# A Mamba-2 scan fused with a low-rank mixer on one core: B, C and y of half the pairs turned as 32x32 squares on VectorE and through DRAM

## The chip, the cores and the metric

The kernel runs on one core of a Trainium2 chip. Its time is the device time of one execution in microseconds (us). Times of single instructions come from one profiled execution, read from the hardware profiler's trace; ns are marked. In the profile's words, PE is TensorE's matmul, PEld its weight load, DVE is VectorE, ACT is ScalarE, POOL is GpSimd, and SP is SyncE, whose queue (SPq) issues the kernel's DMAs.

## The reference, cut to what matters

Two stages follow one another. The first is a chunked scan (Mamba-2): 4 batches, 8 heads, 768 tokens, head dimension 32, state size 16, in chunks of 32 tokens. The second is a mixer on the scan's output, joined over heads to 256 columns: a low-rank mixing over the tokens (rank 32) and a channel MLP (256 to 1024 to 256, with ReLU).

```python
for c in range(seq // 32):                      # per batch and head
    M = (Cc @ Bc.T) * L                         # 32 x 32, decays below the diagonal
    y[c] = M @ xc + (Cc @ state) * exp(cum)     # within the chunk, and from the state
    state = decay_full * state + (Bc * decay_from_j).T @ xc
x = y.transpose(0, 2, 1, 3).reshape(4, 768, 256)
u = x + (x.transpose(0, 2, 1) @ U @ V).transpose(0, 2, 1)
out = u + relu(u @ w_ch1) @ w_ch2
```

All inputs and the output are float32.

## The kernel before, in words

**Tiles.** A batch's 768 tokens are cut into three pairs of two 128-token tiles. The 12 pairs are numbered k = 3 x batch + q. For each pair, B and C (16 columns for each of 8 heads, so 128 columns each) are loaded with tokens on partitions, decayed (`prep`, L463, into BC, and `decayed`, L475), and then turned so that (head, state) lies on the partitions: T holds, for tile i = 0, 1, the turned B and the turned C, 128x128 each. `turning` (L486) does this with four TensorE transposes into one PSUM bank (L497). ScalarE then copies the bank to T (L501) and writes Cm, the turned C under the two masks in `slot` that blank the odd or the even heads (L507). Three T and three Cm tiles are in rotation. `gram` (L521) multiplies B and C of T and Cm into the 32x32 grams, `mask` (L535) lays the causal mask over them, `state` and `update` (L554, L570) carry the state, `inter` (L637) and `intra` (L672) make y, and `yout` (L690) copies it on ScalarE to yT, which holds a batch's y with channels on partitions and tokens along the row: 128 x 2 x 768.

**The mixer of a batch** is made of `project` (L741: y, with tokens on partitions, by U), `mixed` (L755, by V) and `added` (L765, into yT); ScalarE copies what `project` gives to pT (L753), which `mixed` reads. `project` needs y turned back, with tokens on partitions. `ytokening` (L708) does that for a pair: four TensorE transposes into a bank (L714), and one copy of 128x512 to ytok, on ScalarE for batches 0 and 1 and on VectorE for batches 2 and 3. From then on the MLP goes over blocks of 256 tokens, three per batch: `split` (L780) cuts u into a near and a far part and their joint, `first` (L815, eight matmuls and a scaling), `second` (L822, four matmuls and a ReLU) and `third` (L833, two operations of VectorE) make a quarter of the hidden layer in three float32r parts, and `down` (L873) multiplies it by the second weights in pieces. The last pieces of a block add u, turn the result on VectorE in 32x32 squares and write it to the output in four DMAs (`vector.transpose` and L909). Batch 0's blocks are turned by TensorE and written in one DMA of 256 KB (L923), and its blocks 0 and 1 have a plain float32 hidden layer (`plain`, L802), whose pieces of `down` are called plain here, the others split. Every VectorE call is made through one helper, so the profile shows all of them at L169.

**PSUM** has eight banks, in three rotations: "w" 2, "x" 3 and "z" 3 (L130). A bank is handed out again when its last reader is done. The transposes use "w", as do the state and the projection; grams, intra and the MLP use "x" and "z".

**What sets the order.** Nothing is scheduled by a compiler: `follow` (L996) reads a plan, a long string of words, and issues each word's instructions at once, so the words' order is the order on every engine's queue. A word is a letter and numbers. For the scan the number n is the pair k = 3 + n, so that T3 is pair 6, the first of batch 2, and t5 is pair 8. For the mixer, the first number is a lag, and the batch is 1 - lag: f1.2.0 is `first` for batch 0, block 2, quarter 0, p-1 is `project` of batch 2, and p-2 that of batch 3.

| letter | word | engines |
|---|---|---|
| P, D | `prep`, `decayed` | VectorE (GpSimd for batch 0) |
| T (twice per pair) | `turning`: two transposes each; the second also makes the copy and Cm | PE, ACT |
| g; m, M | `gram`; half a mask each | PE; VectorE |
| s; u | `state`; `update` | PE; VectorE, ACT |
| i, n; y | `inter`, `intra`; `yout` | PE; ACT |
| t | `ytokens` | PE, ACT or VectorE |
| L, R, U, c | loads, the weights' splitting, the first weights in plain float32 | SP; VectorE, ACT; PE |
| p; x; a; S | `project`; `mixed`; `added`; `split` | PE, ACT; PE; VectorE; ACT, VectorE |
| f, e, h; d | `first`, `second`, `third`; one piece of `down` or `rows` | PE and ACT, h VectorE |

The engines work their queues in order; a DMA that must wait for something holds SP's queue behind it. The part of the code that decides how T is made, word for word:

```python
def turned(k):
    t = turns.setdefault(k, turning(k))
    for _ in range(2):
        next(t)
```

A T word runs two steps of the generator, up to its second `yield`.

Of the kernel before, what the change touches and what calls it, by code (L numbers as in the profile page):

```python
# [10 lines left out]
FP32 = mybir.dt.float32  # L11
# [3 lines left out]
WCOLS = 512  # L15
NWORDS = 12
PLAIN = 2
ROWS = 3
FOUR = 3

# [3 lines left out]
AF = mybir.ActivationFunctionType  # L24
# [19 lines left out]
        'U1.0.0 g0 U1.0.1 g1 m0 M0 c5 c4 m1 M1 c5 D1 s0 u0 U1.1.0 U1.1.1 U1.1.2 i0 n0 y0 c6 c6 '  # L44
        's1 c5 g2 c7 u1 R2 m2 c7 U1.1.3 M2 c8 c8 c7 U1.0.2 L4 U1.0.3 i1 n1 y1 c6 R1 R0 c8 R5 c9 '
        's2 c9 c9 n2 d1.0 L5 R6 u2 R0 d1.1 P3 S1.2 d1.0 R7 d1.0 i2 y2 R3 t1 R1 t0 R2 R5 d1.1 R4 '
        'f1.2.0 D4 T3 T3 P4 R7 R6 t2 f1.2.1 R3 D3 d1.1 f1.2.2 d1.0 R4 e1.2.0 d1.1 h1.2.0 e1.2.1 '
        'T4 f1.2.3 d1.0 T4 e1.2.2 e1.2.3 h1.2.1 P5 g3 p0 m3 M3 L6 d1.2 d1.2 d1.2 T5 L7 d1.2 L8 '
        'T5 h1.2.2 x0 h1.2.3 d1.2 a0.0 d1.2 d1.2 a0.1 S0.0 d1.2 g4 m4 s3 f0.0.1 D5 M4 f0.0.0 '
        'd1.2 d1.2 d1.2 e0.0.0 e0.0.1 u3 h0.0.0 f0.0.2 d1.2 h0.0.1 f0.0.3 e0.0.2 s4 u4 n3 h0.0.2 '  # L50
        'i3 e0.0.3 h0.0.3 d1.1 D6 S0.1 d1.2 d0.0 d0.0 y3 d0.0 d0.0 d0.0 S0.2 d0.0 d0.0 d0.0 D7 '
        'n4 s5 i4 d0.0 d0.0 g5 P7 y4 u5 P6 m5 M5 d0.0 d0.0 t3 D8 f0.2.1 f0.1.2 s6 n5 i5 y5 '
        'e0.1.2 u6 f0.2.0 f0.1.0 f0.1.3 h0.1.2 T7 e0.2.0 h0.2.0 e0.2.1 e0.1.3 h0.2.1 P8 T7 '
        'h0.1.3 f0.1.1 d0.2 f0.2.2 f0.2.3 e0.1.0 h0.1.0 e0.1.1 h0.1.1 e0.2.2 e0.2.3 h0.2.3 d0.1 '
        'd0.1 T6 T6 d0.1 d0.1 d0.1 t4 h0.2.2 t5 d0.1 d0.1 d0.1 d0.2 d0.2 d0.2 d0.2 d0.0 g7 m7 '
        'p-1 d0.2 d0.2 x-1 M7 a-1.0 a-1.1 s7 d0.2 u7 d0.1 d0.1 d0.1 g6 m6 d0.1 M6 d0.1 d0.2 d0.2 '
        'd0.2 d0.2 d0.2 S-1.0 T8 T8 i6 n6 y6 s8 n7 S-1.1 i7 y7 f-1.0.2 f-1.0.3 g8 e-1.0.2 '
        'e-1.0.3 m8 M8 f-1.1.0 f-1.0.1 h-1.0.3 h-1.0.2 f-1.0.0 f-1.1.1 e-1.1.0 e-1.0.0 e-1.0.1 '
        'h-1.1.0 h-1.0.1 e-1.1.1 f-1.1.2 h-1.0.0 d-1.0 S-1.2 f-1.1.3 e-1.1.2 h-1.1.2 d-1.0 d-1.0 '
        'd-1.0 d-1.0 f-1.2.0 u8 d-1.0 d-1.0 h-1.1.1 d-1.1 e-1.2.0 h-1.2.0 t6 e-1.1.3 f-1.2.2 '  # L60
        'd-1.1 d-1.1 d-1.0 h-1.1.3 e-1.2.2 h-1.2.2 d-1.1 d-1.1 d-1.1 d-1.1 d-1.1 i8 n8 t7 d-1.1 '
        'd-1.1 y8 d-1.1 t8 p-2 d-1.1 x-2 d-1.0 d-1.0 a-2.0 f-1.2.1 a-2.1 S-2.0 d-1.0 d-1.0 S-2.1 '
        'f-1.2.3 e-1.2.1 h-1.2.1 f-2.0.2 e-1.2.3 f-2.0.0 f-2.0.1 d-1.2 d-1.2 e-2.0.0 h-1.2.3 '
        'e-2.0.2 h-2.0.0 f-2.0.3 S-2.2 h-2.0.2 d-1.2 e-2.0.1 d-1.2 d-1.2 d-1.2 e-2.0.3 h-2.0.3 '
        'f-2.1.0 h-2.0.1 f-2.1.1 f-2.1.2 e-2.1.0 e-2.1.1 h-2.1.0 f-2.1.3 d-1.2 d-1.2 d-1.1 '
        'e-2.1.2 h-2.1.1 f-2.2.1 e-2.1.3 d-2.0 d-1.2 d-1.2 d-2.0 d-2.0 d-2.0 h-2.1.2 d-1.2 d-1.2 '
        'd-2.1 d-2.1 d-1.0 h-2.1.3 f-2.2.0 f-2.2.2 d-2.0 d-2.0 d-2.0 d-2.0 e-2.2.2 d-2.1 e-2.2.0 '
        'h-2.2.0 d-1.2 h-2.2.2 d-2.0 d-2.0 f-2.2.3 d-2.1 d-2.1 d-2.1 e-2.2.3 d-2.0 d-2.1 d-2.1 '
        'e-2.2.1 h-2.2.3 d-2.0 d-2.2 d-2.2 d-2.2 d-2.0 h-2.2.1 d-2.1 d-2.1 d-2.1 d-2.1 d-2.2 '
        'd-2.1 d-2.2 d-2.2 d-2.2 d-2.2 d-2.2 d-2.2 d-2.2 d-2.2 d-2.2 '),  # L70
}


# [1 line left out]
def kernel(  # L75
# [37 lines left out]
    NCB = DM // P  # L113
# [4 lines left out]
    NQ = NM // 2  # L118
    Q = 32
# [5 lines left out]
    att = ctx.enter_context(tc.tile_pool(name="att", bufs=2))  # L125
# [32 lines left out]
    class Kept:  # L158
# [6 lines left out]
        def __getattr__(self, name):  # L165
# [8 lines left out]
    vector = Kept(nc.vector)  # L174
# [53 lines left out]
    w1f = [w1all[:, c] for c in range(NQ)]  # L228
# [98 lines left out]
    for g in range(2):  # L327
# [3 lines left out]
        out=la.rearrange("p b c h -> p b h c"),  # L331
# [8 lines left out]
    slot = const.tile([P, 2], FP32)  # L340
# [115 lines left out]
    st = {}  # L456
# [29 lines left out]
    def turning(k, c=0, n=2, tag="w", engine=None, sooner=False):  # L486

        s = st[k]
        if c == 0:
            s["T"] = att.tile([P, 2, 2, P], FP32, tag="T", name="T", bufs=3)  # L490
            s["Cm"] = att.tile([P, 2, 2, P], FP32, tag="Cm", name="Cm", bufs=3)
        tp = bank(tag, 2, n, P)
        for i in range(2):
            for v in range(n):
                if i or v:
                    yield
                nc.tensor.transpose(out=tp[:, i, v],  # L497
                                    in_=s["BC"][:, i, c + v].rearrange("p h n -> p (h n)"),
                                    identity=ident)
        if sooner or not engine:  # L500
            nc.scalar.copy(out=s["T"][:, :, c:c + n], in_=tp)  # L501
        for i in range(2):
            if engine:
                engine.tensor_scalar(out=s["Cm"][:, i, c:c + n], in0=tp[:, 1],
                                     scalar1=slot[:, i, None], scalar2=None, op0=ALU.mult)
            else:
                nc.scalar.activation(s["Cm"][:, i, c:c + n], tp[:, 1], AF.Copy,  # L507
                                     scale=slot[:, i, None])
        if engine and not sooner:
            nc.scalar.copy(out=s["T"][:, :, c:c + n], in_=tp)  # L510
        yield

    def turn(*args):
        for _ in turning(*args):
            pass
# [192 lines left out]
    def ytokening(k, tag="w", copies=None):  # L708

        b, q = pairs[k]  # L710
        t = [bank(tag[0], 2, 2, P)] * 2 if len(tag) == 1 else [bank(n, 2, 2, P) for n in tag]
        for c in range(2):
            for g in range(2):
                nc.tensor.transpose(out=t[c][:, c, g], in_=yT[b][:, g, ts(2 * q + c, P)],  # L714
                                    identity=ident)
            if len(tag) > 1:
                copies[c](out=ytok[b][:, 2 * q + c], in_=t[c][:, c].rearrange("p g d -> p (g d)"))
            yield
        if len(tag) > 1:
            return  # L720
        t = t[0]
        out = ytok[b][:, 2 * q:2 * q + 2].rearrange("p c (g d) -> p c g d", g=2)
        if copies:
            for c in range(2):
                copies[c](out=out[:, c], in_=t[:, c])
        else:
            copy = nc.scalar.copy if b < 2 else vector.tensor_copy
            behind.setdefault("part", copy(out=out, in_=t))
        yield

    def ytokens(*args):
        for _ in ytokening(*args):
            pass


    def mixer(b):
# [136 lines left out]
        def down(j):  # L873
# [9 lines left out]
            t = bank("xz"[j % 2], NCB, HS)  # L883
            if b or j >= PLAIN:
                for v in range(3):
# [45 lines left out]
        def piece(j):  # L931
            next(downs.setdefault(j, (rows if b >= ROWS and j == NBL - 1 else down)(j)))

# [32 lines left out]
    finer, turns = {}, {}  # L966
# [4 lines left out]

    def turned(k):

        t = turns.setdefault(k, turning(k))
        for _ in range(2):
            next(t)

    def crossed(k):

        inter(k, 1)  # L980

    def ytokens_of(k, v):
# [3 lines left out]

    scans = dict(P=prep, D=decayed, T=turned, g=gram, s=state, m=lambda k: mask(k, (0, 1)),
                 M=lambda k: mask(k, (2, 3)), u=update, i=lambda k: inter(k, 0), n=intra,
                 j=crossed, y=yout, t=ytokens, L=load, Q=lambda k, c: prep(k, c, 1),
                 E=lambda k, c: decayed(k, c, 1), O=ytokens_of,  # L990
                 V=lambda k, c, v: turn(k, c, 1, "wx"[v // 2 % 2], vector if v % 2 else None, v > 3))
    whole = dict(c=convert, R=refined, A=lambda i: decays(every_batch, "w", [i]),
# [56 lines left out]
```

## Time and profile before

| what | value |
|---|---|
| device time, 3 runs | 218.95, 219.84, 220.07 us (median 219.84) |
| the profiled execution | 219.55 us, of which its span is 217.8 us |
| PE busy | 205.9 us (95%), 3246 matmuls and transposes |
| DVE busy | 168.3 us (77%), 349 instructions |
| ACT busy | 125.0 us (57%), 287 instructions |
| POOL busy | 6.6 us (3%), 22 instructions |
| DMA | 84,016 packets, 14.60 MB |

The span is the time from the first to the last instruction that the trace holds; the rest of the device time lies around it. Busy shares are shares of the span. The chain of waits is followed back from the last instruction, at each step to whatever released it, or to the instruction ahead of it in its own queue; an engine's share of the chain is the time for which it set the end. Of the idle time before an instruction the profile names what ended it. "issue" there is time for which the engine waited on nothing that the profile shows.

### The profile page before, as it was taken

The numbers are of one execution on the slowest core, as the hardware profiler recorded it, in microseconds if no ns is written. First come the engines' busy times: TensorE is split into PE (matmuls) and PEld (weight loads), VectorE is DVE, ScalarE is ACT, GpSimd is POOL, SyncE is SP. The second block draws the span as 40 slices with busy tenths as digits, with TensorE's granted clock in tenths as the row PEclk, the third lists the DMA queues.
The fourth block names the chain that finished last, engine by engine and source line by source line (L and its number), as shares of the span: only waits on it lengthen the run. The fifth ranks groups of instructions, "written<-read, shape, count | busy, mean of one in ns | idle before, by whom it ended". The sixth has DMA issues, their size and how long they took to land.

```text
span 217.8 us, 7530 instructions
## 1 busy us (share of the span) xinstructions
PE 205.9 (95%) x3246; PEld 185.1 (85%) x3246; DVE 168.3 (77%) x349; ACT 125.0 (57%) x287; POOL 6.6 (3%) x22
## 2 busy tenths in 40 slices
PE   7778799999999999999999999979999999999994
PEld 5555586878879998999999988869999899999993
DVE  3398978998899998699858967847994597874871
ACT  3353749479969774368589513667563276635410
POOL 4132100000000000000000000000000000000000
PEclk9999969999999999999999999999999999999999
DMA  5996789986751017406600020330000000033234
GB/s 82 134 159 178 105 123 225 249 147 157 99 73 26 3 50 97 52 16 87 147 6 0 0 40 14 50 54 0 3 0 3 3 2 0 3 48 51 36 60 96
DMA packets 84016, 14.60 MB, mean 67 GB/s; under 512 B 80336, under 2 KB 82192, under 8 KB 83984
## 3 DMA queue, kind: packets, MB, share of 16 engines
q1 hardware_dynamic: 83984, 14.13, 37.0%
q8 instruction: 25, 0.41, 0.9%
q14 instruction: 7, 0.06, 0.1%
HBM read 10.98 MB, written 3.15 MB: 65 GB/s over the span
## 4 chain that ended last, share of the span: by engine, by line
PE 83%; DVE 6%; ACT 3%; SPq 2%; issue 2%; DMA 2%; POOL 1%; DVEq 0%
PE x L791 35%; PE z L791 28%; PE x L529 3%; SPq L195 2%; PE w L497 2%; PE w L748 2%; PE w L714 2%; DMA bc<-in_B_dram 2%; DVE words L169 2%; PE x L760 2%; PE x L684 1%; PE x L659 1%; PE w L564 1%; PE z L684 1%; DVE M L169 1%
## 5 line engine op out<-in xcount | busy, mean ns | idle before, releaser
L169 DVE SCALAR_TENSOR_TENSOR words<-words 128x512 fp32r<-128x512 f32 (+6 forms) x60 | 39.3, 667 | 4.3 <-PE x L791 1.4
L791 PE MATMUL x<-words,w 128*128 128x256 f32 x288 | 38.3, 280 | 0.0
L791 PEld LDWEIGHTS x<-words,w 128*128 128x128 f32 x288 | 34.9, 188 | 1.8 <-issue 1.7
L791 PE MATMUL z<-u,w 128*128 128x256 f32 x240 | 34.0, 280 | 1.3 <-issue 1.3
L791 PE MATMUL x<-u,w 128*128 128x256 f32 x240 | 34.0, 281 | 0.0
L791 PEld LDWEIGHTS z<-u,w 128*128 128x128 f32 x240 | 30.1, 188 | 1.6 <-issue 1.3
L791 PEld LDWEIGHTS x<-u,w 128*128 128x128 f32 x240 | 30.1, 188 | 0.6 <-issue 0.2
L796 ACT ACTIVATE z<-z 128x512 f32<-128x512 f32 (+1 forms) x24 | 13.9, 578 | 18.0 <-PE z L791 18.0
L796 ACT ACTIVATE x<-x 128x512 f32<-128x512 f32 (+1 forms) x27 | 15.4, 574 | 14.5 <-PE x L791 14.3
L169 DVE SCALAR_TENSOR_TENSOR words<-x,words 128x512 fp32r<-128x512 f32 x20 | 13.7, 685 | 10.7 <-ACT words L831 10.5
L791 PE MATMUL z<-words,w 128*128 128x256 f32 x144 | 19.3, 280 | 0.0
L791 PEld LDWEIGHTS z<-words,w 128*128 128x128 f32 x144 | 17.5, 188 | 0.4 <-issue 0.4
L831 ACT ACTIVATE words<-z 128x512 fp32r<-128x512 f32 x20 | 11.8, 601 | 6.1 <-PE x L791 4.3
L831 ACT ACTIVATE words<-x 128x512 fp32r<-128x512 f32 x20 | 11.8, 600 | 4.8 <-PE x L791 4.7
L169 DVE SCALAR_TENSOR_TENSOR words<-z,words 128x512 fp32r<-128x512 f32 x20 | 13.6, 679 | 1.2 <-ACT words L831 1.2
L169 DVE SCALAR_TENSOR_TENSOR S<-S,kept,w 128x64 f32<-128x64 f32 x40 | 11.2, 279 | 1.6
L169 DVE TENSOR_TENSOR BC<-bc,F 128x512 f32<-128x512 f32 (+2 forms) x18 | 8.9, 508 | 4.2 <-DMA bc<-in_B_dram 2.8
L169 DVE TENSOR_TENSOR M<-x,causal 128x256 int32<-128x256 int32 x24 | 9.0, 417 | 3.8 <-PE z L529 3.8
L169 DVE TENSOR_TENSOR yT<-x,yT 128x384 f32<-128x384 f32 (+1 forms) x15 | 9.2, 612 | 3.2 <-PE z L760 3.1
L596 ACT ACTIVATE Sm<-S,slot 128x128 f32<-128x128 f32 (+1 forms) x18 | 6.1, 386 | 9.1 <-DVE S L169 9.1
L529 PE MATMUL x<-Cm,T 32*64 32x128 f32 x192 | 9.4, 307 | 1.7 <-DVE Cm L169 1.7
L659 PE MATMUL z<-T,Sm 32*64 32x64 f32 x180 | 7.7, 239 | 2.1 <-DVE settled L169 2.0
(152 smaller groups left out, 377.5 us busy)
## 6 DMA issues: line engine op xcount, KB each, us to landing
words<-in_moe_w_ch_dram SPq DMA_DIRECT2D x7, 512.0 KB, 5.9
x<-in_x_dram SPq DMA_DIRECT2D x24, 128.0 KB, 3.9
out_dram<-o SPq DMA_DIRECT2D x32, 64.0 KB, 2.2
bc<-in_B_dram SPq DMA_DIRECT2D x24, 64.0 KB, 3.3
bc<-in_C_dram SPq DMA_DIRECT2D x12, 128.0 KB, 3.7
out_dram<-words SPq DMA_DIRECT2D x3, 256.0 KB, 3.2
words<-in_moe_w_ch_dram SPq DMA_DIRECT2D x2, 256.0 KB, 4.8
out_dram<-o SPq DMA_DIRECT2D x2, 128.0 KB, 1.8
```

The lines of the kernel that those rows point to most:

```text
L169: self.last = call(*args, **kwargs)
L195: op = nc.sync.dma_start(**kwargs)
L497: nc.tensor.transpose(out=tp[:, i, v], in_=s["BC"][:, i, c + v].rearrange("p h n -> p (h n)"), identity=ident)
L529: nc.tensor.matmul(out=g[r][cols, c], lhsT=s["T"][rows, 0, c, cols], rhs=s["Cm"][rows, :, :, ts(2 * c + p, Q)].rearrange("r v t i -> r v i ...
L596: nc.scalar.activation(s["Sm"][:, sl, v], s["S"][:, sl, ts(v, D)], AF.Copy, scale=slot[:, v, None])
L659: product = nc.tensor.matmul(out=y[r // 2][p][ts(v, H), c], lhsT=own[ts(r, Q)], rhs=s["T"][ts(r, Q), 1, :, ts(2 * c + p, Q)].rearrange("r ...
L684: product = nc.tensor.matmul(out=y[n][p][ts(v, Q), c], lhsT=x_sb[k][half, c, h], rhs=s["M"][half, h // 2, c, h % 2], start=fresh(k, n, p, ...
L714: nc.tensor.transpose(out=t[c][:, c, g], in_=yT[b][:, g, ts(2 * q + c, P)], identity=ident)
L748: nc.tensor.matmul(out=p[ts(n, H)], lhsT=UU[:, c].rearrange("p t r -> p (t r)"), rhs=ytok[b][:, c, ts(n, P)], start=(c == 0), stop=(c == N ...
L791: nc.tensor.matmul(out=t, lhsT=lhsT, rhs=rhs, start=start, stop=True, skip_group_check=True)
L796: nc.scalar.activation(t, t, AF.Copy, scale=1.0 + EPS)
L831: nc.scalar.activation(gs[j, i][0], t, AF.Relu, scale=NEAR)
```

## The change

For the pairs of batches 2 and 3 (k from SQUARED = 6 on) the two turnings are done in another way. The first T word issues one VectorE transpose of the whole BC tile, 128x512, in 32x32 squares, each turned in place of its own partitions, into a tile `w1f` of the first weights in float32 (one of the four, in turn; the weights in it are used up), and four SP DMAs (`send`), each taking 32 partitions to a DRAM buffer in pieces of 32 numbers. The second T word issues one SP DMA (`fetch`) that reads the buffer into T, held until the four sends are done, and the two Cm of ScalarE, which now read T and not a bank. ScalarE's copy to T goes. Likewise for y: the first t word issues two VectorE transposes of 128x256 from yT and the four sends, and the second t word issues the fetch into ytok; the copy to ytok on VectorE goes. Each of the twelve turnings has a DRAM buffer of its own. In the plan, T words stay two per pair and t words of batches 2 and 3 become two per pair. The plan is the same up to "d1.1 R4" in its eleventh line, and in another order from there on. The diff, with the middle of the plans left out:

```diff
@@ -15,6 +15,7 @@
 WCOLS = 512
 NWORDS = 12
 PLAIN = 2
+SQUARED = 6
 ROWS = 3
 FOUR = 3
 
@@ -44,30 +45,30 @@
         'U1.0.0 g0 U1.0.1 g1 m0 M0 c5 c4 m1 M1 c5 D1 s0 u0 U1.1.0 U1.1.1 U1.1.2 i0 n0 y0 c6 c6 '
         's1 c5 g2 c7 u1 R2 m2 c7 U1.1.3 M2 c8 c8 c7 U1.0.2 L4 U1.0.3 i1 n1 y1 c6 R1 R0 c8 R5 c9 '
         's2 c9 c9 n2 d1.0 L5 R6 u2 R0 d1.1 P3 S1.2 d1.0 R7 d1.0 i2 y2 R3 t1 R1 t0 R2 R5 d1.1 R4 '
-        'f1.2.0 D4 T3 T3 P4 R7 R6 t2 f1.2.1 R3 D3 d1.1 f1.2.2 d1.0 R4 e1.2.0 d1.1 h1.2.0 e1.2.1 '
-        'T4 f1.2.3 d1.0 T4 e1.2.2 e1.2.3 h1.2.1 P5 g3 p0 m3 M3 L6 d1.2 d1.2 d1.2 T5 L7 d1.2 L8 '
-        'T5 h1.2.2 x0 h1.2.3 d1.2 a0.0 d1.2 d1.2 a0.1 S0.0 d1.2 g4 m4 s3 f0.0.1 D5 M4 f0.0.0 '
...
-        'h0.1.3 f0.1.1 d0.2 f0.2.2 f0.2.3 e0.1.0 h0.1.0 e0.1.1 h0.1.1 e0.2.2 e0.2.3 h0.2.3 d0.1 '
-        'd0.1 T6 T6 d0.1 d0.1 d0.1 t4 h0.2.2 t5 d0.1 d0.1 d0.1 d0.2 d0.2 d0.2 d0.2 d0.0 g7 m7 '
-        'p-1 d0.2 d0.2 x-1 M7 a-1.0 a-1.1 s7 d0.2 u7 d0.1 d0.1 d0.1 g6 m6 d0.1 M6 d0.1 d0.2 d0.2 '
-        'd0.2 d0.2 d0.2 S-1.0 T8 T8 i6 n6 y6 s8 n7 S-1.1 i7 y7 f-1.0.2 f-1.0.3 g8 e-1.0.2 '
-        'e-1.0.3 m8 M8 f-1.1.0 f-1.0.1 h-1.0.3 h-1.0.2 f-1.0.0 f-1.1.1 e-1.1.0 e-1.0.0 e-1.0.1 '
-        'h-1.1.0 h-1.0.1 e-1.1.1 f-1.1.2 h-1.0.0 d-1.0 S-1.2 f-1.1.3 e-1.1.2 h-1.1.2 d-1.0 d-1.0 '
-        'd-1.0 d-1.0 f-1.2.0 u8 d-1.0 d-1.0 h-1.1.1 d-1.1 e-1.2.0 h-1.2.0 t6 e-1.1.3 f-1.2.2 '
-        'd-1.1 d-1.1 d-1.0 h-1.1.3 e-1.2.2 h-1.2.2 d-1.1 d-1.1 d-1.1 d-1.1 d-1.1 i8 n8 t7 d-1.1 '
...
+        'P4 T3 f1.2.0 R7 d1.1 f1.2.1 T4 e1.2.0 R3 f1.2.2 R6 h1.2.0 d1.1 e1.2.1 h1.2.1 f1.2.3 '
+        'd1.0 e1.2.2 e1.2.3 T3 t2 T4 L6 P5 h1.2.2 d1.2 d1.2 d1.2 T5 g3 m3 M3 p0 d1.0 D3 x0 R4 '
+        'h1.2.3 d1.2 d1.1 a0.0 a0.1 d1.2 d1.2 d1.2 d1.2 s3 g4 m4 d1.2 d1.2 d1.2 S0.0 f0.0.0 u3 '
+        'd1.2 f0.0.1 e0.0.0 f0.0.2 P6 T5 L7 d1.2 e0.0.1 e0.0.2 M4 D4 n3 s4 i3 h0.0.0 y3 f0.0.3 '
+        'D5 h0.0.1 u4 T6 n4 s5 e0.0.3 h0.0.2 t3 i4 y4 d0.0 d0.0 d0.0 h0.0.3 d0.0 d0.0 P7 S0.1 '
...
+        'f0.2.2 f0.2.3 e0.1.1 d0.2 e0.2.2 e0.2.3 d0.1 T6 d0.1 u6 h0.1.3 d0.2 D8 d0.2 d0.1 d0.2 '
+        'h0.2.0 h0.2.1 h0.1.1 h0.1.0 d0.1 d0.1 d0.1 d0.1 t4 d0.2 P8 t3 T8 d0.1 h0.2.2 s7 h0.2.3 '
+        'd0.2 d0.2 d0.1 u7 d0.1 d0.1 d0.2 T7 d0.1 g6 s8 u8 m6 M6 d0.2 d0.2 d0.2 d0.2 i6 t4 t5 n6 '
+        'y6 p-1 g7 T8 x-1 d0.2 d0.1 m7 M7 a-1.0 n7 a-1.1 S-1.0 t6 i7 g8 m8 M8 t6 y7 S-1.1 '
+        'f-1.0.2 f-1.0.1 n8 i8 y8 e-1.0.2 f-1.1.2 f-1.0.0 f-1.1.1 e-1.1.2 e-1.0.0 f-1.0.3 '
+        'e-1.0.1 h-1.0.2 f-1.1.0 t8 d-1.0 e-1.0.3 h-1.0.0 h-1.0.1 f-1.1.3 d-1.0 d-1.0 t7 h-1.0.3 '
+        'd-1.0 d-1.0 e-1.1.0 e-1.1.1 h-1.1.0 S-1.2 e-1.1.3 d-1.0 d-1.0 d-1.1 d-1.0 d-1.1 f-1.2.0 '
+        'h-1.1.2 d-1.0 d-1.0 t8 d-1.0 d-1.1 h-1.1.1 d-1.0 t7 p-2 d-1.1 x-2 d-1.1 h-1.1.3 a-2.0 '
+        'd-1.1 S-2.0 d-1.1 d-1.1 e-1.2.0 h-1.2.0 f-1.2.2 d-1.1 f-1.2.1 a-2.1 e-1.2.2 f-2.0.0 '
+        'd-1.1 d-1.1 f-2.0.2 e-1.2.1 h-1.2.2 e-2.0.0 h-1.2.1 f-1.2.3 d-1.1 S-2.1 f-2.0.1 e-1.2.3 '
...
 }
 
 
@@ -508,6 +509,60 @@
                                      scale=slot[:, i, None])
         if engine and not sooner:
             nc.scalar.copy(out=s["T"][:, :, c:c + n], in_=tp)
+        yield
+
+    turns_by = {}
+
+    def squares(key):
+
+        n = len(turns_by)
+        turns_by[key] = n
+        t = w1f[n % NQ].rearrange("p c m -> p (c m)")
+        d = nc.dram_tensor(f"squares{n}", [Q, 4, 4 * P], FP32, kind="Internal").ap()
+        return t, d
+
+    def send(sq, d):
+
+        return [nc.sync.dma_start(
+            out=d.rearrange("x g (w a t) -> a x (g w) t", w=4, a=4)[r],
+            in_=sq[ts(r, Q)].rearrange("x (w t) -> x w t", t=Q)) for r in range(4)]
+
+    def fetch(dst, d, sent):
+
+        op = nc.sync.dma_start(out=dst, in_=d.rearrange("x g w -> g x w"))
+        for s in sent:
+            hold(op, s)
+
+    def squared(k):
+
+        s = st[k]
+        s["T"] = att.tile([P, 2, 2, P], FP32, tag="T", name="T", bufs=3)
+        s["Cm"] = att.tile([P, 2, 2, P], FP32, tag="Cm", name="Cm", bufs=3)
+        sq, d = squares(("T", k))
+        vector.transpose(
+            out=sq.rearrange("p (g w t) -> p w g t", g=4, w=4),
+            in_=s["BC"].rearrange("p i c h n -> p (i c) (h n)").rearrange(
+                "p w (g t) -> p w g t", g=4))
+        sent = send(sq, d)
+        yield
+        yield
+        fetch(s["T"].rearrange("p i c t -> p (i c t)"), d, sent)
+        for i in range(2):
+            nc.scalar.activation(s["Cm"][:, i], s["T"][:, 1], AF.Copy, scale=slot[:, i, None])
+        yield
+        yield
+
+    def squaring(k):
+
+        b, q = pairs[k]
+        sq, d = squares(("y", k))
+        for n in range(NCB):
+            vector.transpose(
+                out=sq.rearrange("p (e c n x) -> p n c e x", e=4, c=2, n=2)[:, n],
+                in_=yT[b][:, n, ts(q, 2 * P)].rearrange("p (c e x) -> p c e x", c=2, e=4))
+        sent = send(sq, d)
+        yield
+        fetch(ytok[b][:, 2 * q:2 * q + 2].rearrange("p c d -> p (c d)"), d, sent)
         yield
 
     def turn(*args):
@@ -971,9 +1026,18 @@
 
     def turned(k):
 
-        t = turns.setdefault(k, turning(k))
+        t = turns.setdefault(k, (squared if k >= SQUARED else turning)(k))
         for _ in range(2):
             next(t)
+
+    sides = {}
+
+    def sided(k):
+
+        if k < SQUARED:
+            ytokens(k)
+        else:
+            next(sides.setdefault(k, squaring(k)))
 
     def crossed(k):
 
@@ -986,7 +1050,7 @@
 
     scans = dict(P=prep, D=decayed, T=turned, g=gram, s=state, m=lambda k: mask(k, (0, 1)),
                  M=lambda k: mask(k, (2, 3)), u=update, i=lambda k: inter(k, 0), n=intra,
-                 j=crossed, y=yout, t=ytokens, L=load, Q=lambda k, c: prep(k, c, 1),
+                 j=crossed, y=yout, t=sided, L=load, Q=lambda k, c: prep(k, c, 1),
                  E=lambda k, c: decayed(k, c, 1), O=ytokens_of,
                  V=lambda k, c, v: turn(k, c, 1, "wx"[v // 2 % 2], vector if v % 2 else None, v > 3))
     whole = dict(c=convert, R=refined, A=lambda i: decays(every_batch, "w", [i]),
```

## The prediction

> **What bounds the kernel now.** I read the page's first two parts, then the table of windows, the chain of waits in order of time, the groups by form, and the DMA issues. Two rows of the 40 slices and the chain's summary:
>
> ```profile
> PE   7778799999999999999999999979999999999994
> DVE  3398978998899998699858967847994597874871
> PEclk9999969999999999999999999999999999999999
> ...
> PE 83%; DVE 6%; ACT 3%; SPq 2%; issue 2%; DMA 2%; POOL 1%; DVEq 0%
> ```
>
> TensorE (PE) is at 9 in every slice but one from the eighth on, at the full granted clock. Windows (columns: stretch, length, then busy time of PE, PEld, DVE, ACT, POOL, granted clock, DMA share, GB/s) show it in the reordered part:
>
> ```profile
> 60.00:70.00 10.00, 9.84 (x91) 8.47 (x90) 9.72 (x19) 7.95 (x20) 0.00 (x0) 1.00 0.40 54
> 70.00:80.00 10.00, 10.00 (x95) 9.20 (x93) 9.60 (x16) 8.10 (x17) 0.00 (x0) 1.00 0.01 2
> ...
> 130.00:140.00 10.00, 9.91 (x292) 8.37 (x293) 8.06 (x18) 3.99 (x12) 0.00 (x0) 1.00 0.17 28
> 140.00:150.00 10.00, 8.74 (x139) 8.12 (x135) 5.63 (x11) 6.82 (x17) 0.00 (x0) 1.00 0.28 44
> ```
>
> The words of both orders agree up to d1.1 and R4, which TensorE reaches at 65.0 us. From there PE idles for 0.09 + 1.26 us in all. The 1.26 stands in the middle of a word's matmuls, and no semaphore ends it ("issue" in the chain):
>
> ```profile
> 121.56 0.44 PE w L497 x4
> ...
> 142.07 1.26 issue
> ...
> 165.88 0.59 PE w L714 x4
> ```
>
> So the end is set by the sum of TensorE's work; what leaves TensorE counts in full unless something new comes late. VectorE (DVE) has no room from 60 to 80 us (9.7 and 9.6 of 10).
>
> **The change, part by part.** *Removed from TensorE:* for six pairs, four transposes of B and C (L497) and four of y (L714): 48. The chain shows four in 0.44 us (0.59 at 165.88), as they follow one another. 12 x 0.44 = 5.3 us; with 0.59, 7.1. All else in TensorE's queue after 65 us is the same words in another order. I take 5.3.
>
> *VectorE.* The groups (columns: busy, mean ns | idle before):
>
> ```profile
> L169 DVE STREAM_TRANSPOSE o<-yT 128x512 f32<-128x512 f32 x8 | 5.6, 705 | 0.1
> L169 DVE COPY ytok<-w 128x512 f32<-128x512 f32 x6 | 4.1, 685 | 3.1 <-PE w L714 3.1
> L501 ACT COPY T<-w 128x512 f32<-128x512 f32 x9 | 5.3, 592 | 4.7 <-PE w L497 4.5
> ```
>
> Neighbours in its timeline start some 0.08 us before the last one's end, so 705 ns costs 0.63 and the copy 0.60. It gains six turns of 128x512 (3.8) and twelve of 128x256, and loses six copies (3.6). A 128x256 turn isn't in the trace: two masks of that size take 0.66 to 0.75 together, two turns of full size 1.26. I take 0.7 (the half-size row is the nearest), so 4.2 in all. Sum +4.4 (+7.8 by the dear end): 173 to 176 of 212, below TensorE; what counts is where they fall.
>
> *ScalarE (ACT)* loses six copies of T (0.47 each, start to start). Its two Cm per pair stay, but now wait for a DMA instead of a bank, and all that ScalarE has behind them waits too.
>
> *SP and DMA.* Twelve tiles each get four sends of 64 KB in 512 pieces of 128 B, and one fetch of 256 KB (128 pieces of 2 KB). The output of batches 1 to 3 already goes out with the first shape, batch 0's with 256 KB (columns after the colon: SP's min/median/max ns for one issue):
>
> ```profile
> L909 SPq DMA_DIRECT2D out_dram<-o x32: 590/627/1975, 127.2 to 213.6; - x32
> ...
> out_dram<-o SPq DMA_DIRECT2D x32, 64.0 KB, 2.2
> out_dram<-words SPq DMA_DIRECT2D x3, 256.0 KB, 3.2
> ```
>
> SP: 48 x 0.627 + 12 x 0.42 = 35 us of issuing, and each fetch holds SP until its sends land. From the end of a turn, with SP free: the fourth send begins after 3 x 0.63 = 1.9, lands 2.2 later (4.4 is the longest of the 32), and the fetch takes another 3.2 (4.8 is the 256 KB load of weights, under load): 7.3 us, 11.1 at the dear end, and 5.5 if both land in the 1.8 of the quickest output row. I take 7.3 where SP is free, since these rows have the same bytes and pieces. Traffic: 26,112 packets. Queue 1 spent 37.0% of 217.8 us on 16 engines for 83,984 packets, 15.3 ns each; 26,112 / 16 x 15.3 ns = 25 us per engine, spread from 70 to 157 us, where the DMA row is mostly 0 to 6 of 10. I add nothing for it, up to 1 or 2 us per round trip if it collides with x's loads.
>
> [...]
>
> **What is late next.** I walked the four queues of the new order by hand, each word at its start-to-start time in the old trace (f 0.91, e and a split d piece 0.45, a plain d piece 1.73, a VectorE 128x512 0.61, a dependent pair 1.33):
> 1. T3 and T4 are turned among R7, R3 and R6 from 68.8 on. The add that frees the bank of the first d1.2 piece stands on VectorE behind P4, two turns, R7, R3, R6, h1.2.0 and h1.2.1 (the first half of h): .61 + 2 x .63 + 5 x 1.33, and the add itself .62, so to 77.9 or later; TensorE comes at 77.8. Wait 0.9.
> 2. T3's turn ends at 70.1. SP issues its sends to 72.6, T4's to 75.1, and only then fetches T3, which lands at 78.5; Cm is done at 79.5. Gram g3 comes at 80.0, so the margin is 0.5. T4's fetch holds ScalarE to 81.8, and pT, which x0 needs, stands behind it: 0.3.
> 3. a0 and the banks of g4 at 85 to 89: 0.1.
> 4. At 124.4, d0.2 needs h0.2.3, behind turns t4, P8, T8 on VectorE: 0.9.
> 5. From 131 to 142: p-1 (132.5) needs t5's fetch (131.7, margin 0.8); y6 waits for yT behind VectorE's turns, g7 for y6's copies, x-1 for m7 and M7: 1.7 in all.
> 6. p-2 (159.0) needs t7's fetch (158.1, margin about 1). Past 161 I found no wait.
>
> New waits: 0.9 + 0.3 + 0.1 + 0.9 + 1.7 = 3.9 us. The old waits (0.09 + 1.26) belong to the old order; I take them out, though the 1.26 has no cause that I can see and may come again.
>
> **Sum.** The profiled run took 219.55 us: a span of 217.8 and 1.75 around it. 219.55 - 5.3 - 1.35 + 3.9 = 216.8. That run is 0.3 below the median of three (219.84), which is less than the runs' spread, so 216.8 stands for the median.
>
> **Rivals.**
> *The waits aren't there* (VectorE catches up, as it does in the old 76 to 80 us, where its adds wait for TensorE): 219.55 - 5.3 = 214.3, and 213.0 if the 1.26 goes too. For it: only 6% of the chain is VectorE now. Against it: items 1 and 4 put whole turns ahead of work that TensorE needs within 2 us. Chance 0.13.
>
> *It is given back at the edges*: the hand walk is right in kind, but each round trip is 1 us longer than its bounds allow for (a send's landing at 3.2) and the 1.26 stays, so the gain ends as 219 to 220. Chance 0.15.
>
> *The round trip is late at its users: slower.* Three users have margins of 0.5 (g3, with ScalarE stuck behind Cm), 0.8 (p-1) and 1.0 (p-2). If the trip takes d more than 7.3, TensorE loses (d - 0.5) + (d - 0.8) + (d - 1.0) = 3d - 2.3. At d = 1.7 the 2.75 gained are gone, from d = 2.0 it is slower by over 0.5%; at d = 3 (10.3, inside the 11.1) it adds 6.7: 223.5. For it: nothing in the old order waits for a round trip, and 4.4 us is seen for the same send. Against it: median 2.2, and the DMA engines are at 0 to 4 tenths in those places. Chance 0.28 for all d of 2.0 and above. [...]
>
> *The change doesn't do what it says* (the time of the transposes was idle TensorE time anyway, 219.5 as before): the windows at 10.00 of 10 speak against it; 0.02, counted with "same".
>
> **Chances and range.** 0.42 for the forecast (215.5 to 218.2), 0.13 for the full gain, 0.17 for no difference, 0.28 for slower. 0.5% of 219.84, about what can be told from no change, is 1.1 us: faster is below 218.7, slower above 220.9. The range leaves out the lower half of the full gain and about the upper third of the slower cases: 214.0 to 223.2. The forecast's own range is 215.5 to 218.2.
>
> **What would show it.** Right: L497's f32 128x128 transposes fall from 40 to 16 and L714's from 40 to 16; PE's busy time falls by 5 to 7 us; VectorE's rises to 172 or 173 us; sends land in 2.2 and fetches in 3.2; PE's idle time after 65 us is 3 to 5 us, most of it ended by VectorE, at about 78, 124 and 131 to 138 us. Wrong: idle time of PE ended by ScalarE's Cm or by a DMA into T or ytok at g3, p-1 or p-2 (the slower rival); turns well above 705 ns or a 128x256 turn at 600 or more, which puts 0.3 to 0.7 us per pair on VectorE from 66 to 92 us; sends that land in 4 us; or an idle stretch of PE without releaser, as at 142 us.

## The result, and the profile after

The changed kernel takes 236.42 us (median of six runs, 234.92 to 239.57) against 220.24 (218.95 to 221.4) before: a ratio of 1.0725, 95% interval 1.0663 to 1.0786. The forecast was 216.8; the measured time lies outside its range, on the third rival's side and well past that rival's 223.5. The profiled execution has a span of 235.0 us. Its rows of PE, granted clock and DMA, and the chain's summary:

```profile
PE   7788699999999869999999981899996999999994
PEclk9979979999999979999999996558999999999999
DMA  6984888985453357265573433422231000230224
...
PE 58%; DMA 14%; DVE 13%; SPq 6%; ACT 4%; issue 3%; DVEq 0%; ACTq 0%
```

PE has two holes, a shallow one (82 to 88 us) and one down to a tenth (141 to 147), and the granted clock stands at half behind the second. DMA, 2% of the chain before, is now 14%, of which the fetches are 9%. TensorE's waits from 60 us on (engine, tile, line, awaited: us in total, times, longest):

```profile
PE w L803 <- DMA ytok<-squares: 8.3, 3, 5.0
PE x L584 <- ACT Cm L551: 2.6, 1, 2.6
PE z L846 <- DVE words L170: 0.2, 1, 0.2
PE x L846 <- DVE o L170: 0.2, 1, 0.2
```

L803 is `project`, L584 `gram`. The waits sit at g3 (2.64), p-1 (5.04 and 1.52) and p-2 (1.77), the three places of the third rival. VectorE ends 0.4 us in all. The chain in order of time names what was late (start, length, what):

```profile
77.98 5.12 DMA T<-squares
...
137.63 10.17 DMA ytok<-squares
```

It is the fetches, 5.1 and 10.2 us where I had 3.2. The sends did what the output's row had promised:

```profile
squares<-w1f SPq DMA_DIRECT2D x48, 64.0 KB, 2.2
```

What a fetch does is seen in windows of 1 us (columns as in the prediction's windows; the last three are granted clock, DMA share, GB/s). At 80, 81, 143 and 146 us next to nothing moves but fetches; the other two lines are for the clock, below:

```profile
80.00:81.00 1.00, 1.00 (x11) 1.00 (x10) 1.00 (x3) 0.34 (x1) 0.00 (x0) 1.00 0.26 94
81.00:82.00 1.00, 0.45 (x4) 0.25 (x3) 0.96 (x2) 0.00 (x0) 0.00 (x0) 1.00 0.26 98
...
85.00:86.00 1.00, 1.00 (x14) 1.00 (x14) 1.00 (x4) 0.00 (x0) 0.00 (x0) 0.54 0.35 63
...
143.00:144.00 1.00, 0.00 (x0) 0.00 (x0) 0.00 (x0) 0.95 (x6) 0.00 (x0) 0.55 0.26 96
146.00:147.00 1.00, 0.33 (x4) 0.00 (x0) 0.00 (x0) 0.00 (x0) 0.00 (x0) 0.50 0.26 100
155.00:156.00 1.00, 1.00 (x31) 0.90 (x30) 0.79 (x3) 0.93 (x5) 0.00 (x0) 0.50 0.00 0
```

Work is queued and waited for, yet the 16 DMA engines are busy for 0.26 of the time: four of sixteen, at 94 to 100 GB/s together. The packet records of the trace agree: while the fetches' pieces of 2 KB move, 3.5 to 3.8 are in flight on the mean (9 to 13 for the other transfers in 2 KB pieces), a single fetch moves for 3.0 to 4.1 us, and the four issued from 135.9 to 138.6 moved for 12.2 us, one behind the other. `fetch` walks the buffer as 4 groups of 32 rows, so its outermost dimension is 4; that of `send` is 32.

The same windows show a second cost. TensorE stands still from 81.4 to 84.1 us and, but for one short burst, from 140.2 to 147.9, and the granted clock falls to half at 85.07 (0.54 in that window) and at 143.10 (0.55). It comes back at 88.49 and, the second time, only at 160.17, though PE is recorded as busy again from 147.9 on.

These four times lie 1, 16 and 5 steps of 3.41 us apart. In every run's trace the clock changes on such a grid, whose place differs from run to run (in that of before it falls at 28.53 us and rises at 31.94). Cut at the grid, the changed kernel's waits look like this:

```profile
81.66:85.07 3.41, 0.99 (x36) 0.76 (x38) 1.38 (x3) 1.38 (x3) 0.00 (x0) 1.00 0.59 132
85.07:88.49 3.42, 3.42 (x32) 2.76 (x28) 3.38 (x8) 1.17 (x3) 0.00 (x0) 0.50 0.57 78
139.69:143.10 3.41, 0.48 (x8) 0.24 (x6) 0.82 (x2) 1.44 (x5) 0.00 (x0) 1.00 0.37 119
177.23:180.65 3.42, 1.70 (x18) 1.33 (x17) 2.84 (x5) 0.00 (x0) 0.00 (x0) 1.00 0.22 83
```

In the first and third line PE is idle for 2.4 and 2.9 us of the step, and the clock is at half from the step's end on. The wait at p-2 (fourth line) leaves 1.7 us of one step idle, and the clock stays. In all runs, from 40 us on, each of the 13 steps at full clock with 1.8 us or more of idle PE was followed by half clock, and of the 13 with 1.1 to 1.75 us one was (1.6 us, in e3).

### The profile page after: what moved, and what is told of

Read it like the earlier page. It is cut to its first block, busy times and chain, and to the rows that moved or that the text cites. A ratio compares the mean times of both kernels' runs of the same rounds, so it can differ in the third digit from the quotient of the medians.

```text
span 235.0 us, 7537 instructions
## 1 busy us (share of the span) xinstructions
PE 213.2 (91%) x3198; PEld 188.9 (80%) x3198; DVE 172.7 (73%) x361; ACT 123.4 (53%) x281; POOL 6.6 (3%) x22
## 4 chain that ended last, share of the span: by engine, by line
PE 58%; DMA 14%; DVE 13%; SPq 6%; ACT 4%; issue 3%; DVEq 0%; ACTq 0%
PE x L846 23%; PE z L846 18%; DMA ytok<-squares 7%; DVE words L170 6%; DMA bc<-in_B_dram 4%; SPq L196 4%; PE x L584 3%; DMA T<-squares 2%; PE w L803 2%; PE x L815 2%; DVE w1f L170 1%; SPq L526 1%; PE x L739 1%; DVE BC L170 1%; DVE w L170 1%
## 5 line engine op out<-in xcount | busy, mean ns | idle before, releaser
L846 PE MATMUL x<-words,w 128*128 128x256 f32 x288 | 39.5, 282 | 0.1
L846 PEld LDWEIGHTS x<-words,w 128*128 128x128 f32 x288 | 35.8, 189 | 1.3 <-issue 0.8
L846 PEld LDWEIGHTS z<-u,w 128*128 128x128 f32 x240 | 31.0, 193 | 0.8 <-DVE words L170 0.4
L846 PEld LDWEIGHTS x<-u,w 128*128 128x128 f32 x240 | 31.0, 193 | 0.6 <-ACT yT L759 0.3
L170 DVE SCALAR_TENSOR_TENSOR words<-x,words 128x512 fp32r<-128x512 f32 x20 | 13.6, 682 | 12.2 <-ACT words L886 12.1
L846 PE MATMUL z<-words,w 128*128 128x256 f32 x144 | 19.9, 280 | 0.0
L851 ACT ACTIVATE z<-z 128x512 f32<-128x512 f32 (+1 forms) x24 | 13.7, 573 | 10.6 <-PE z L846 10.2
L846 PEld LDWEIGHTS z<-words,w 128*128 128x128 f32 x144 | 18.0, 188 | 0.7 <-issue 0.7
L803 PE MATMUL w<-ytok,UU 128*64 128x128 f32 x72 | 7.3, 356 | 8.3 <-DMA ytok<-squares 8.3
L584 PE MATMUL x<-Cm,T 32*64 32x128 f32 x192 | 11.2, 336 | 3.9 <-ACT Cm L551 2.6
L551 ACT ACTIVATE Cm<-T,slot 128x256 f32<-128x256 f32 x12 | 5.4, 500 | 15.8 <-DMA T<-squares 15.8
L803 PEld LDWEIGHTS w<-ytok,UU 128*64 128x64 f32 x72 | 5.3, 176 | 9.7 <-DMA ytok<-squares 9.2
```

Of the source, the lines that this page charges most:

```text
L170: self.last = call(*args, **kwargs)
L551: nc.scalar.activation(s["Cm"][:, i], s["T"][:, 1], AF.Copy, scale=slot[:, i, None])
L584: nc.tensor.matmul(out=g[r][cols, c], lhsT=s["T"][rows, 0, c, cols], rhs=s["Cm"][rows, :, :, ts(2 * c + p, Q)].rearrange("r v t i -> r v i ...
L803: nc.tensor.matmul(out=p[ts(n, H)], lhsT=UU[:, c].rearrange("p t r -> p (t r)"), rhs=ytok[b][:, c, ts(n, P)], start=(c == 0), stop=(c == N ...
L846: nc.tensor.matmul(out=t, lhsT=lhsT, rhs=rhs, start=start, stop=True, skip_group_check=True)
L851: nc.scalar.activation(t, t, AF.Copy, scale=1.0 + EPS)
```

## The experiments

**Theory A**: a fetch runs on four DMA engines, for its outermost dimension; so it lands late, fetches queue behind one another, TensorE waits, and the clock is halved behind the waits. **Rival B**: the sends in pieces of 128 B and the traffic are what is slow. **Rival C**: the new order and VectorE's load cost the time. **Rival D**, formed after the first runs: SP, which issues all of it, is the bound of the trip.

**e1_fetch4: the fetch in four DMAs.** Same buffer, same pieces; each DMA has 32 as its outermost dimension.

```diff
-        op = nc.sync.dma_start(out=dst, in_=d.rearrange("x g w -> g x w"))
-        for s in sent:
-            hold(op, s)
+        for g in range(4):
+            op = nc.sync.dma_start(out=dst[ts(g, Q)], in_=d[:, g])
+            for s in sent:
+                hold(op, s)
```

> The changed kernel with each fetch cut into four DMAs of 32 rows (64 KB each) in place of one whose outermost dimension is 4. Theory A (a fetch runs on only four of the sixteen DMA engines, so it lands in 5 us alone and in 10 behind others): the landing falls to about 3 us, the waits of TensorE for Cm and ytok (2.6 and 8.3 us) fall below 2 us in all, the granted clock stays near 1, and the time is 216 to 220. Rival B (the sends in pieces of 128 B and the traffic make the round trip late): the fetches are no earlier, 232 or more. Rival C (the new order costs the time): no change, 234 to 238.

229.05 us (ratio 1.0393, 1.0343 to 1.0443): 7 us better, but not 216 to 220. In most of its stretches of fetching 7 to 9 pieces of 2 KB are in flight (some 4 in the two with gaps), the DMA share is 0.47 to 0.53 (windows from 138 to 139 and 140 to 142 us) where the changed kernel had 0.26, and each quarter lands quickly:

```profile
T<-squares SPq DMA_DIRECT2D x24, 64.0 KB, 2.1
ytok<-squares SPq DMA_DIRECT2D x24, 64.0 KB, 2.1
```

So more than four engines work on it, as A has it. But 36 more issues of 0.42 us stand in SP's queue, 16 of them from 135.4 to 143.8 us, just when p-1 (137.7) waits for ytok: 4.3 us of waiting are left there, 2.0 at g3, and the half clock with them. Hence rival D.

**e2_order, e3_t_only, e4_y_only: the order alone, and each half.** All turnings, or those of y, or those of B and C, go back to TensorE.

```diff
# e2, e4: B and C on TensorE, all at the first T word
-        t = turns.setdefault(k, (squared if k >= SQUARED else turning)(k))
-        for _ in range(2):
-            next(t)
+        t = turns.setdefault(k, turning(k))
+        for _ in range(2 if k < SQUARED else 4):
+            next(t, None)
# e2, e3: y on TensorE, at the first t word (pairs 6 and 8: at the second)
-        else:
-            next(sides.setdefault(k, squaring(k)))
+        elif sides.setdefault(k, k not in (6, 8)):
+            if sides[k] != 2:
+                ytokens(k)
+            sides[k] = 2
+        else:
+            sides[k] = 1
```

> The new order alone: all twelve turnings back on TensorE and a bank, T at its first word, y at its first word too (at its second for pairs 6 and 8, where a bank is not free at the first). Theories A and B: the order by itself costs little, 218 to 223, no DMA wait of TensorE. Rival C: 230 or more.

> B and C by squares and DRAM as in the changed kernel, y on TensorE. Theory A: the 2.6 us before the first gram and the slower clock behind it stay, the 8.3 us of waits for ytok and the half clock behind them (about 6 us) go, 2.6 us of transposes come back: about 224. Rival B: half of the sends are left, about 228. Rival C: 235.

> y by squares and DRAM as in the changed kernel, B and C on TensorE. Theory A: the wait before the first gram and its slow clock go (-4.3), 2.6 us of transposes come back; the fetches into ytok no longer share four engines with those of T, so the wait before the projection of batch 2 falls from 6.6 to 2 to 4 us, with or without the half clock: 225 to 232. Rival B: about 228. Rival C: 235.

232.65 (ratio 1.0559, 1.0506 to 1.0613), 231.94 (1.0476, 1.0397 to 1.0555) and 227.76 us (1.0303, 1.0234 to 1.0373). e4 is in A's range, e3 is 8 us above it, and e2, at full clock and with no wait for a DMA, looks like rival C. The three longest of its waits from 60 us on (6.8 us in all) say what it is:

```profile
PE w L498 <- DVE S L170: 2.0, 1, 2.0
PE w L619 <- ACT Cm L508: 1.8, 2, 1.1
PE x L846 <- DVE words L170: 1.4, 1, 1.4
```

L498 and L619 are the transposes of B and C and `state`, which both need a bank "w", in an order that was made for turnings without a bank. So these three tell little of the changed kernel: each brings waits of its own, and the halves don't add up. Rival C needed a run with the order untouched.

**e5_no_trip: no round trip, all else the same.** The fetch reads the input x, ahead of the sends, and waits for nothing.

```diff
-        op = nc.sync.dma_start(out=dst, in_=d.rearrange("x g w -> g x w"))
-        for s in sent:
-            hold(op, s)
+        nc.sync.dma_start(out=dst, in_=x[0].rearrange("h s d -> (h s d)")[:P * 4 * P].rearrange(
+            "(p w) -> p w", w=4 * P))
...
+        fetch(s["T"].rearrange("p i c t -> p (i c t)"), d, None)
         sent = send(sq, d)
         yield
         yield
-        fetch(s["T"].rearrange("p i c t -> p (i c t)"), d, sent)
```

> The changed kernel with the same turns and sends, but each fetch issued ahead of its sends, at the first word, from 256 KB of the input x in one straight DMA of 128 rows that waits for nothing. (T and y's turned copy hold other numbers, so the output is not the reference's.) Theory A (the round trip that comes late, and the slow clock that follows, are the whole loss): no wait of TensorE for Cm or ytok, clock 1, 215 to 219, as the forecast had it. Rival C (the order and VectorE's load cost the time): 225 or more.

216.22 us (ratio 0.9786, 0.9711 to 0.9861). All turns, all 48 sends and the order are in it, and TensorE waits from 60 us on for no DMA:

```profile
PE x L814 <- ACT pT L807: 0.6, 1, 0.6
PE x L738 <- issue: 0.3, 1, 0.3
PE z L845 <- DVE words L170: 0.2, 1, 0.2
PE x L845 <- DVE o L170: 0.2, 1, 0.2
```

Rivals B, as far as traffic goes, and C fall: the trip's lateness and what follows from it are the whole loss. Since no fetch waits for a send here, the run says nothing on rival D.

**e6_busy and e10_busy2: TensorE kept busy while it waits.** Idle matmuls of the identity ahead of g3, p-1 and p-2, by the plan's F word: F24, F72, F16 in e6, F11, F28, F7 in e10.

```diff
- ... L6 P5 h1.2.2 d1.2 d1.2 d1.2 T5 g3 m3
+ ... L6 P5 h1.2.2 d1.2 d1.2 d1.2 T5 F24 g3 m3
...
-y6 p-1 g7
+y6 F72 p-1 g7
```

> The changed kernel with idle matmuls of the identity put where TensorE waits: 24 ahead of g3, 72 ahead of p-1, 16 ahead of p-2 (0.11 us each). They delay nothing but the waiting. If the half clock at 85 to 88 and 143 to 160 us follows from TensorE's idle time: the clock stays near 1 and 6 to 8 us are won, 228 to 230. If it does not: the clock's row is as before, 236 to 238.

> e6_busy with the idle matmuls sized by what one took there (0.22 us, not 0.11): 11 ahead of g3, 28 ahead of p-1, 7 ahead of p-2, so that they fill the waits of the changed kernel (2.6, 6.6 and 1.8 us) and no more. If the half clock comes of TensorE's idle time: clock near 1 and 5 to 8 us less than the changed kernel, 228 to 231; the waits themselves stay as idle matmuls. If it does not: 236.

e6: 243.28 us (ratio 1.1037, 1.0965 to 1.1109). One identity product took 0.22 us (the trace shows it as two matmuls), not the 0.11 that I had taken from the transposes, so the fill ran longer than the waits (16.3 us at p-1). For the clock the run is good all the same:

```profile
PEclk9979999999999999999999999999999999999999
```

No slice is at half from 40 us on. From p-1's start to n8's the same words took 8.9 us; in the changed kernel 20.4, of which 6.6 was waiting: the half clock had cost 4.9 us there. e10, with the fill sized to the waits: 231.86 us (ratio 1.0532, 1.0455 to 1.0609), 4.6 below the changed kernel, a little less than the 5 to 8 expected. In its trace, too, the clock stays at 1.00 from 40 us to the last slice, although TensorE still stands for 2.7 us at g3, behind the fill (83.0 to 85.7). That wait falls across two steps of the clock's grid, which have 1.4 and 1.3 us of idle PE:

```profile
81.04:84.45 3.41, 2.00 (x11) 1.60 (x9) 1.08 (x2) 0.00 (x0) 0.00 (x0) 1.00 0.55 133
84.45:87.86 3.41, 2.14 (x56) 1.79 (x56) 1.28 (x4) 1.88 (x5) 0.00 (x0) 1.00 0.27 64
```

In these two runs the clock does follow TensorE's idle time, and the steps of 1.4 and 1.3 us did not halve it.

**e7_pool: the fetches on GpSimd's queue.**

```diff
-        op = nc.sync.dma_start(out=dst, in_=d.rearrange("x g w -> g x w"))
+        op = nc.gpsimd.dma_start(out=dst, in_=d.rearrange("x g w -> g x w"))
```

> The changed kernel with the twelve fetches issued by GpSimd in place of SP, so that they hold no sends up. Theory A: the fetch itself still has its outermost dimension of 4; if GpSimd's queue spreads it no better, it still lands 5 us and more after its issue, but is not behind T8's sends: 230 to 235. If GpSimd's queue cuts it over all DMA engines, 218 to 224.

238.56 us (ratio 1.0817, 1.0746 to 1.0889), worse than both forecasts. SP is free of the fetches, but they land in a median of 5.9 us (T) and 6.2 (ytok) after their issue; TensorE waits for Cm, ytok and pT 12.0 us in all. Relieving SP without a faster fetch won nothing here.

**e8_early: the old order, eight turnings, with much time for the trip.** T of pairs 9 to 11 and y of pairs 6 to 10 go by squares; each T has three words there (send, fetch, Cm).

```diff
-M5 d0.0 d0.0 t3 D8 f0.2.1 f0.1.2 s6 n5 i5 y5 e0.1.2 u6 f0.2.0
+M5 d0.0 d0.0 T7 t3 D8 f0.2.1 f0.1.2 s6 n5 i5 y5 e0.1.2 u6 T6 t4 f0.2.0
-P8 T7 h0.1.3 f0.1.1 d0.2 f0.2.2 f0.2.3 e0.1.0
+P8 T8 t3 h0.1.3 f0.1.1 d0.2 t5 f0.2.2 T6 t4 f0.2.3 e0.1.0
```

> The old order with eight of the twelve turnings by squares: T of pairs 9 to 11 and y of pairs 6 to 10, each sent as soon as its source is there, fetched some 5 us later and used 8 us or more later still, Cm in a word of its own. Theory A (what fails is the trip's lateness at its users): 8 x 0.44 = 3.5 us less, 216 to 218, clock 1. Rival B (sends in pieces of 128 B and the traffic slow other work): 221 or more.

232.48 us (ratio 1.0539, 1.0464 to 1.0613): a clear miss. I had spaced the words by TensorE's time and not by SP's: sixteen sends in a row hold SP from 108.4 to 120.3 us, so T7's fetch, whose sends were out by 111.6, starts at 120.3. Then ScalarE stands:

```profile
ACT Cm L551 <- DMA T<-squares: 13.3, 2, 7.1
```

**e9_layout: one fetch with 128 rows outermost.** The buffer's dimensions change places, so that a fetch has 128 rows as its outermost dimension (four pieces of 512 B each) and stays one DMA. Turns, sends and waits keep their number and place.

```diff
-        d = nc.dram_tensor(f"squares{n}", [Q, 4, 4 * P], FP32, kind="Internal").ap()
+        d = nc.dram_tensor(f"squares{n}", [4, 4, Q, P], FP32, kind="Internal").ap()
-            out=d.rearrange("x g (w a t) -> a x (g w) t", w=4, a=4)[r],
+            out=d.rearrange("w g x (a t) -> a x (w g) t", a=4)[r],
-        op = nc.sync.dma_start(out=dst, in_=d.rearrange("x g w -> g x w"))
+        op = nc.sync.dma_start(out=dst.rearrange("p (w m) -> p w m", w=4),
+                               in_=d.rearrange("w g x m -> (g x) w m"))
-            out=sq.rearrange("p (g w t) -> p w g t", g=4, w=4),
+            out=sq.rearrange("p (w g t) -> p w g t", g=4, w=4),
-                out=sq.rearrange("p (e c n x) -> p n c e x", e=4, c=2, n=2)[:, n],
+                out=sq.rearrange("p (c n e x) -> p n c e x", e=4, c=2, n=2)[:, n],
```

> The changed kernel with the DRAM buffer laid out as [4 column blocks, 4 groups, 32, 128 numbers] in place of [32, 4, 512], so that one fetch has 128 rows as its outermost dimension (512 pieces of 512 B) and stays one DMA. Turns, sends, waits and order are as in the changed kernel. Theory A (the fetch's four engines are the root, through the late landings and the slow clock behind them): the fetch lands in 2.5 to 4 us, the waits for Cm and ytok fall below 2 us in all, clock near 1, 216 to 219. Rival D (the trip is late whatever the fetch, since SP's queue issues 48 sends one behind the other): waits of 4 us and more at p-1 with the half clock behind it, 225 to 230.

216.84 us (six runs, 215.32 to 218.23) against 219.88 before: ratio 0.987, 0.9814 to 0.9926. It is faster than both kernels, than the one before by 1.3%. Its fetches, its PE row and its waits of TensorE from 60 us on:

```profile
T<-squares SPq DMA_DIRECT2D x6, 256.0 KB, 3.7
ytok<-squares SPq DMA_DIRECT2D x6, 256.0 KB, 3.0
```

```profile
PE   7787869999999999999999999899999999999994
PEclk9969979999999999999999999999999999999999
```

```profile
PE x L816 <- ACT pT L809: 0.6, 1, 0.6
PE z L847 <- DVE words L170: 0.2, 1, 0.2
PE x L847 <- DVE o L170: 0.2, 1, 0.2
PE x L740 <- issue: 0.2, 1, 0.2
```

From 78 to 79 us, with the fetches of T3 and T4 issued, the DMA engines are busy for 0.55 of the time, at 161 GB/s (0.26 and 98 GB/s in the changed kernel from 81 to 82). Both holes are gone and the clock stays. Theory A holds, and rival B falls, since the 48 sends in pieces of 128 B are still there. Rival D falls only in part, for the new layout also made SP's issues shorter (min/median/max ns for one send, in the changed kernel and in e9):

```profile
L526 SPq DMA_DIRECT2D squares<-w1f x48: 549/627/1951, 72.0 to 171.8; - x48
...
L526 SPq DMA_DIRECT2D squares<-w1f x48: 302/494/1862, 71.7 to 155.6; - x48
```

No run separates the two. My estimate puts e9's landings (3.6 us after issue for the first fetch into T, 3.2 and 4.4 for the last two into ytok ahead of p-1) behind the changed kernel's issue times: Cm would be done at 82.5 where TensorE comes at 81.4, and ytok be there at 140.3 and 142.0 where it comes at 140.2. So 1.1 us of waiting would be left at g3, 0.7 at p-1 and none at p-2, 1.8 of the 11.0. The fetch is by far the larger part.

**e11_early_layout: e8 with e9's layout** (the two edits above together).

> e8_early with the buffer's layout of e9_layout: the old order, eight turnings by squares, fetches over all DMA engines. If what went wrong in e8_early was the fetch's four engines too: 216 to 219, as e8_early was meant to give. If it was SP, which there issues sixteen sends in a row (108 to 120 us) and so starts every fetch some 8 us late: Cm and ytok still come late, 224 to 230.

222.53 us (ratio 1.0104, 0.999 to 1.0218), between the two: 10 of e8's 12 us over before go with the layout, that is, with what it does to the fetch and with SP's shorter issues (the sixteen sends in a row took 10.5 us, 11.9 in e8). ScalarE still waits 6.1 us for T, TensorE 2.4 for ytok; the sixteen sends, still ahead of the first fetch, are the likely cause, but no run shows it.

## Why the prediction was wrong, point by point

The changed kernel and e9 issue the same words in the same order, so the starts of the words show where 19.2 us of span went (235.0 against 215.7):

| from | to | changed | e9 | longer by | of it |
|---|---|---|---|---|---|
| start | g3 | 84.1 | 81.0 | 3.0 | wait 2.6 |
| g3 | x0 | 4.3 | 3.0 | 1.3 | half clock |
| x0 | p-1 | 51.1 | 51.2 | -0.1 | |
| p-1 | g7 | 9.4 | 1.5 | 7.9 | waits 6.6, half clock 1.4 |
| g7 | n8 | 11.0 | 7.6 | 3.4 | half clock |
| n8 | p-2 | 18.3 | 18.2 | 0.1 | |
| p-2 | x-2 | 4.1 | 2.1 | 2.0 | wait 1.8 |
| x-2 | end | 52.6 | 51.1 | 1.5 | open |

Waits are 11.0, the clock some 6. (From g7 to n8, e9 has a wait of 0.6 for pT that the changed kernel hasn't.) The last 1.5 isn't explained: PE is at 10.00 of 10 in both, with 87 to 89 matmuls recorded per 10 us against 90 or 91.

*The step that failed* is "the fetch takes another 3.2", in the price of the round trip: I took it from the row of `out_dram<-words`, because bytes and pieces were alike, and did not look at the shape of the DMA. That row is a write with 128 partitions outermost; the fetch reads with 4 outermost. T3's took 5.1 us; those with no other fetch beside them took 4.4 to 5.4, from issue to the end of the last packet. And I did not think of fetches that queue behind one another, which at p-1 made it 10.2. From the end of T3's turn (71.95) to Cm (83.12) the trip was 11.2 us where the walk had 8.4 (70.1 to 78.5): 6.0 up to the fetch's issue, behind eight sends, where it had 5.0, and 5.1 for the fetch, where it had 3.4. In e9 the same stretch is 8.3 us (71.6 to 79.9), 4.6 up to the issue and 3.6 for the fetch. So of the 2.9 us that T3's trip is shorter there, about half is the fetch and half SP; at p-1 nearly all is the fetch.

That the outermost dimension sets the number of engines is inferred from three shapes: with 4 outermost the DMA share was 0.26, with e1's 32 it was 0.47 to 0.53, with e9's 128 it was 0.55. e1 has four DMAs in place of one and e9 has smaller pieces (512 B), so no run varied that dimension alone.

*The third rival* had the places right (g3, p-1, p-2), and its sum 3d - 2.3 gives 9.1 us for the d of 3.8 that its own dear end allowed, against 11.0 measured. That the sums are so near is in part luck, for its terms are 3.3, 3.0 and 2.8 us and the waits were 2.6, 6.6 and 1.8: the fetches that queue at p-1 are not in it. (One slip: at d = 2.0 it gives 220.5 us, only 0.3% over before; 0.5% needs a d of 2.15.) The rival's 223.5 was too low for another reason: it left out the half clock behind the waits, some 6 us. The full clock came back one step of 3.41 us after the wait at g3 (85.07 to 88.49), but after the one at p-1 only behind 12 us of PE recorded as busy at 0.50 (148 to 160).

*The pieces of 128 B* did not show as a price: a send of 64 KB in them landed in 2.2 us, e1's quarter of a fetch, 64 KB in pieces of 2 KB, in 2.1.

*What was right:* the transposes' two groups fell from 40 to 16 each; VectorE's busy time is 172.7 us (forecast 172.7), its turn 705 ns and the pair of half turns 0.76; a send lands in 2.2 and takes SP 0.627.

*What was right by luck, in part:* e9, where a fetch lands in 3.0 to 3.7 us, came to 216.84 against the 216.8 of the sum. But the hand walk has 3.9 us of new waits, most of them ended by VectorE. In e9 only some 1 us of idle TensorE is seen after 60 us, and none at 78 or 124. e9's reordered part began 1.5 us later than that of before (f1.2.0 at 68.1 against 66.6), with no word changed ahead of it. The cause is open; e9's clock row dips in two slices ahead of 60 us, that of before in one. From there to the end it is 3.6 us shorter (147.6 against 151.2) with waits of about the same size, so by this estimate what left TensorE was worth some 3.5 us there, not 5.3. The errors of the terms made up for one another. PE's busy time fell by 2.0 us (205.9 to 203.9), not by 5 to 7: its ends are modelled, and it was a poor test.

## What to carry to other kernels

Price a DMA by a row with the same direction and the same outermost dimension, not by its bytes: a buffer in DRAM has a layout, and the one whose read begins with a dimension of 4 left the DMA engines idle for 0.74 of the time, twelve of sixteen, at no saving anywhere (256 KB landed in 4.4 to 5.4 us with no other fetch beside it, and in a median of 3.0 to 3.7 in e9). A DMA share that stood still at 0.26, while TensorE waited for the DMA, was the sign. And price a wait of TensorE with what follows it: here 11.0 us of waits brought some 6 us of half clock, and it mattered how much of a wait fell into one step of 3.41 us.

## What the runs showed of the hardware that I had not expected

- One DMA with an outermost dimension of 4 moved 94 to 100 GB/s at a DMA share of 0.26, that is on some four of the 16 engines, 24 GB/s each; 256 KB by it took 3.0 to 4.1 us of moving, and four at once took 12.2 us with 3.7 pieces in flight on the mean.
- The clock changed on a grid of 3.41 us. It was halved at the end of a step with 1.8 us or more of idle PE, even where work had come back 1.0 us earlier (idle 81.4 to 84.1, halved at 85.07), and it stayed at 0.50 for 12 us in which PE was recorded as busy (148 to 160), with small matmuls among them.
- A send of 512 pieces of 128 B took SP 0.627 us with one layout of the DRAM buffer and 0.494 with the other. Why was not tested.
- An identity product of 128x128 took 0.22 us as a matmul, recorded as two of 0.11; a transpose of that size is recorded as one (four in 0.44).
- Issued by GpSimd, the same fetch landed in 5.9 to 6.2 us. On how many engines it ran was not settled.
